# Turning early query and key tiles with 64x64 products, fewer halved first products, and a new step table, in a chunked attention + gated FFN kernel

## Chip, cores and metric

One NeuronCore of one Trainium2 chip runs the whole kernel. The metric is the device time of one execution in microseconds (us), from repeated runs; the kernel before takes 471.27 us (median of 3 runs, 470.78 to 471.43).

## What is computed

Batch 8, sequence 576, 8 heads of 64, model width 512, inner width 1024, all float32:

```python
def _attn_ref(q, k, v):              # attention inside chunks of 64 rows, 9 chunks a sequence
    scores = scale * np.matmul(q_c, k_c.transpose(0, 1, 2, 4, 3))
    scores = scores - np.max(scores, axis=-1, keepdims=True)
    attn = np.exp(scores)
    attn = attn / (np.sum(attn, axis=-1, keepdims=True) + 1e-09)
    out = np.matmul(attn, v_c)

def _moe_ref(x, w_in, conv_w, w_out):
    h = np.maximum(x @ w_in, 0.0)
    for k in range(K):               # a 3-tap convolution along the sequence, per inner feature
        conv_out += conv_w[k][None, None, :] * hp[:, k:k + S, :]
    gate = 1.0 / (1.0 + np.exp(-conv_out))
    return (h * gate @ w_out).astype(np.float32)
```

The attention output, heads side by side, is the `x` of the second function. `w_in`, `conv_w` and `w_out` reach the kernel as float64 and are split there.

## The kernel before

The 4608 rows are 36 tiles of 128 (two chunks each), and four tiles are a unit (9 units of 512 columns).

**Attention of a tile.** `load_rows` (L111) brings q and k, `t_pe` (L169) turns them on PE so that the 64 head features lie along partitions, `t_copy` (L189) brings the result from PSUM, `scores` (L206) multiplies, `s_max`, `s_sub`, `s_exp`, `s_sum`, `s_eps`, `s_rec`, `s_norm` (L222 to L275) make the softmax (DVE, with the exponential on ACT and the last product on POOL), `p_pe` and `p_copy` turn it, `attn_v` (L294) multiplies with v, and `x_hi`, `x_lo` (L325, L328) split the result into two fp32r parts, `x_h` and `x_l`. The first five tiles (t < `NP`) have q and k interleaved in one row buffer `r`: even partitions hold q, odd ones k, each partition two sequence rows. One step `t_pe` takes the rows of one parity (i is 0 or 1) of q and k: 8 products of 128 rows by 64 columns of weights over a 128-column stride-two view of the identity; two steps make a tile. Tiles 0 to 3 go through scores one by one, later ones in pairs.

**Feed-forward.** `mm1` (L332) makes 12 products per unit u and feature group f of 128 (8 groups) from `wi_h`, `wi_l`, `x_h`, `x_l`. Unit 0's are cut into two halves of 256 columns, so that the first half can begin when only tiles 0 and 1 are there. ReLU, the three taps (`c_mid`, `c_left` L378, `c_right` L384), the gate (`c_sig`, `c_mul` L394) and the split of the gated result (`g_hi`, `g_lo`) follow, then `mm2` (L465), three products for a block of 128 output rows and one f, stored by `o_store`.

**Weights.** `split` takes each float64 weight apart with `w_scale` (ACT), `w_shift` (L516) and `w_words` (L521) on DVE, `w_hi` (ACT, DVE L560 or POOL L563) and `w_left` (L525, DVE or POOL).

**Order.** Every operation is a step with an engine and assumed cost. A list of numbers, `order_`, gives the order in which the steps are laid out, and `moved_` puts some steps on another engine than their first. The code runs through the list with its assumed costs, hands out buffers and PSUM banks, emits the instructions, and then ties the order of each engine to what was emitted: every engine works strictly in that order, DMA issues (all on SP) too. Where that run leaves more than 0.7 us of the first 110 us between two PE steps, products of the identity with itself are put in (L1018 of 512 columns, L1021 of 128), into a bank that is free then. They compute nothing that is used.

## Time and profile before

| what | us |
|---|---|
| median of the runs | 471.27 |
| profiled execution | 470.57 |
| its span, first to last instruction | 468.8 |
| PE busy | 460.9 (98%) |
| DVE busy | 350.3 (75%) |
| ACT busy | 226.6 (48%) |
| POOL busy | 184.6 (39%) |

Busy time counts an instruction from its start to its modelled end. Matmuls overlap each other, so a group's busy sum on PE can exceed the time it takes; differences between start times show what a step takes. The profile counts each float32 product that goes through the array twice as two records: a step of 8 products in `t_pe` is 16 records, one of 16 products in `scores` 32.

### The profile page before, as it was taken

Reading aid. Unit: us, or ns where it says so; the run is one execution under the profiler, and the core shown is the slowest. Engines: PE = TensorE matmul, PEld = TensorE weight load, DVE = VectorE, ACT = ScalarE, POOL = GpSimd, SP = SyncE. Lnnn points to the kernel's source line nnn. Section 1 sums busy time; section 2 is a strip of 40 time slices with the busy share of each in tenths; the row PEclk is TensorE's granted clock in tenths of the full one; section 3 lists DMA queues with packets and bytes.
Section 4 is the critical chain, followed back from the end, with each engine's and each line's share of the span. In section 5 each row is a group of like instructions: output and inputs, shape, how many; then the busy total and the mean of one; then the engine's idle time right before and its main releaser. Section 6 shows DMA issues by size and latency. Waiting matters only on the chain.

```text
span 468.8 us, 10873 instructions
## 1 busy us (share of the span) xinstructions
PE 460.9 (98%) x4373; PEld 384.1 (82%) x4373; DVE 350.3 (75%) x632; ACT 226.6 (48%) x522; POOL 184.6 (39%) x256
## 2 busy tenths in 40 slices
PE   8999999999999999999999999999999999999996
PEld 6789978888888888888888888888888888888885
DVE  2999998699879947995997868894799178436630
ACT  3678964365347524651365435444355076115521
POOL 1224645067145630674064625272345246203230
PEclk9999999999999999999999999999999999999999
DMA  8998979957469514759496488602230103101002
GB/s 212 250 317 247 279 81 128 149 95 95 96 110 146 135 57 72 167 89 146 101 144 78 67 135 154 119 1 70 60 99 3 45 1 112 46 1 69 1 22 112
DMA packets 175638, 50.53 MB, mean 108 GB/s; under 512 B 159180, under 2 KB 167908, under 8 KB 175588
## 3 DMA queue, kind: packets, MB, share of 16 engines
q1 hardware_dynamic: 175588, 49.85, 55.4%
q8 instruction: 34, 0.56, 0.5%
q14 instruction: 16, 0.13, 0.1%
HBM read 36.72 MB, written 9.44 MB: 98 GB/s over the span
## 4 chain that ended last, share of the span: by engine, by line
PE 89%; DVE 9%; issue 2%; ACT 0%; POOL 0%; POOLq 0%; DVEq 0%; ACTq 0%
PE b_ps L469 42%; PE b_ps L337 37%; PE b_ps L215 3%; PE b_ps L303 3%; PE b_ps L176 2%; DVE wt L521 1%; DVE x_l L329 1%; DVE z L245 1%; DVE ww L521 1%; DVE m L225 1%; DVE wi_l L525 1%; DVE c L378 1%; DVE wt L516 1%; DVE e L229 1%; DVE c L394 1%
## 5 line engine op out<-in xcount | busy, mean ns | idle before, releaser
L469 PE MATMUL b_ps<-wo_h,g_h 128*128 128x512 f32 x288 | 113.8, 395 | 0.3 <-DVE x_l L329 0.3
L469 PE MATMUL b_ps<-wo_h,g_l 128*128 128x512 f32 x288 | 112.2, 390 | 0.0
L469 PE MATMUL b_ps<-wo_l,g_h 128*128 128x512 f32 x288 | 112.2, 390 | 0.0
L417 POOL TENSOR_TENSOR g_l<-c,g_h 128x510 fp32r<-128x510 f32 (+1 forms) x80 | 79.4, 998 | 75.4 <-DVE g_h L406 48.5
L378 DVE SCALAR_TENSOR_TENSOR c<-b_ps,cw,c 128x510 f32<-128x510 f32 x72 | 53.2, 740 | 37.4 <-ACT c L373 30.8
L337 PE MATMUL b_ps<-x_h,wi_h 128*128 128x512 f32 (+1 forms) x320 | 79.8, 371 | 0.0
L337 PE MATMUL b_ps<-x_l,wi_h 128*128 128x512 f32 (+1 forms) x320 | 78.8, 368 | 0.0
L337 PE MATMUL b_ps<-x_h,wi_l 128*128 128x512 f32 (+1 forms) x320 | 78.7, 368 | 0.0
L337 PEld LDWEIGHTS b_ps<-x_h,wi_h 128*128 128x128 f32 x320 | 56.5, 188 | 10.6 <-issue 0.3
L337 PEld LDWEIGHTS b_ps<-x_l,wi_h 128*128 128x128 f32 x320 | 56.9, 188 | 10.1
L337 PEld LDWEIGHTS b_ps<-x_h,wi_l 128*128 128x128 f32 x320 | 56.9, 189 | 10.0
L469 PEld LDWEIGHTS b_ps<-wo_h,g_h 128*128 128x128 f32 x288 | 54.0, 188 | 12.4 <-DVE x_l L329 0.7
L469 PEld LDWEIGHTS b_ps<-wo_h,g_l 128*128 128x128 f32 x288 | 54.1, 188 | 11.4
L469 PEld LDWEIGHTS b_ps<-wo_l,g_h 128*128 128x128 f32 x288 | 54.1, 188 | 10.7
L373 ACT ACTIVATE c<-b_ps,cw 128x510 f32<-128x510 f32 (+1 forms) x72 | 49.8, 693 | 23.0 <-DVE b_ps L348 19.1
L344 ACT ACTIVATE b_ps<-b_ps 128x512 f32<-128x512 f32 x56 | 32.4, 584 | 55.2 <-PE b_ps L337 54.7
L260 POOL TENSOR_TENSOR wt<-wt,z 128x512 f32<-128x512 f32 x28 | 29.2, 1050 | 75.7 <-DVE z L251 28.0
L390 ACT ACTIVATE c<-c 128x510 f32<-128x510 f32 (+1 forms) x72 | 45.5, 635 | 27.7 <-DVE c L384 27.4
L394 DVE SCALAR_TENSOR_TENSOR c<-c,b_ps 128x510 f32<-128x510 f32 (+1 forms) x72 | 48.6, 678 | 10.2 <-ACT c L390 8.1
L384 DVE SCALAR_TENSOR_TENSOR c<-b_ps,cw,c 128x510 f32<-128x510 f32 (+1 forms) x72 | 53.0, 740 | 1.6 <-ACT rim L363 0.4
L201 DVE STREAM_TRANSPOSE qkT<-qk 128x512 f32<-128x512 f32 (+1 forms) x60 | 37.9, 641 | 2.8 <-DMA qk<-in_k 1.5
L326 ACT CAST x_h<-b_ps 128x512 fp32r<-128x512 f32 x36 | 20.6, 590 | 39.6 <-PE b_ps L303 36.0
(99 smaller groups left out, 504.4 us busy)
## 6 DMA issues: line engine op xcount, KB each, us to landing
out<-os SPq DMA_DIRECT2D x35, 256.0 KB, 2.3
qk<-in_k SPq DMA_DIRECT2D x24, 288.0 KB, 6.8
qk<-in_q SPq DMA_DIRECT2D x24, 288.0 KB, 5.9
v<-in_v SPq DMA_DIRECT2D x25, 256.0 KB, 3.3
w<-in_moe_w_out SPq DMA_DIRECT2D x4, 1024.0 KB, 7.3
wt<-wt SPq DMA_DIRECT2D x56, 64.0 KB, 2.0
v<-in_v SPq DMA_DIRECT2D x20, 128.0 KB, 4.4
w<-in_moe_w_in SPq DMA_DIRECT2D x2, 1024.0 KB, 7.0
```

The lines of the kernel that those rows point to most:

```text
L201: nc.vector.transpose(out=turned(st)[:, i].rearrange("p g (n i) -> p g n i", i=32)[:, :, to:to + n], in_=groups[b, i][:, :, n0:n0 + n, :])
L260: nc.gpsimd.tensor_tensor(out=two(st, "to"), in0=two(st, "of"), in1=z, op=ALU.mult)
L326: nc.scalar.copy(out=x_view(t, x_h), in_=x_src(st))
L337: nc.tensor.matmul(banks[st["h"]][:, c0:c1], lhsT=wt[:, f // 2, kt, P * (f % 2):P * (f % 2) + P], rhs=xt[:, u % 2, kt, c0:c1], start=n == ...
L344: nc.scalar.activation(out=h, in_=h, func=AF.Relu)
L373: nc.scalar.mul(out=st["c"], in_=banks[st["h"]][:, i0:i0 + n], mul=cw[:, FT + f:FT + f + 1])
L378: nc.vector.scalar_tensor_tensor(out=c[:, a:n], in0=banks[st["h"]][:, i0 + a - 1:i0 + n - 1], scalar=cw[:, f:f + 1], in1=c[:, a:n], op0=AL ...
L384: nc.vector.scalar_tensor_tensor(out=st["c"], in0=banks[st["h"]][:, i0 + 1:i0 + 1 + n], scalar=cw[:, 2 * FT + f:2 * FT + f + 1], in1=st["c ...
L390: nc.scalar.activation(out=st["c"], in_=st["c"], func=AF.Tanh, scale=0.5)
L394: nc.vector.scalar_tensor_tensor(out=st["c"], in0=st["c"], scalar=1.0, in1=banks[st["h"]][:, i0:i0 + n], op0=ALU.add, op1=ALU.mult)
L417: nc.gpsimd.tensor_tensor(out=g_l[:, f, gs], in0=st["c"][:, cs], in1=g_h[:, f, gs].bitcast(F32), op=ALU.subtract)
L469: nc.tensor.matmul(banks[st["o"]], lhsT=gt[:, f, o:o + P], rhs=wt[:, f, :], start=f == 0 and n == 0, stop=f == FT - 1 and n == 2)
```

## The change

A step `t_pe64` replaces the two `t_pe` steps of tiles 0 to 4: q lies in partitions 0 to 63 and k in 64 to 127, each product takes a 64x64 block of one of them over a 64x64 identity, 32 products in all, q's into one PSUM bank and k's into another. `t_copy` reads the new layout. Unit 0's `mm1` is halved for groups 0, 1, 6 and 7 only. `s_eps`, the addition of 1e-9 on 128x8 values, may go to POOL (21 of 36 do). Assumed transfer times are changed, and `order_` and `moved_` are new throughout. Filler products differ where the gaps of the assumed run differ.

```diff
+    HALVED = (0, 1, 6, 7)
...
     def load_rows(st, t):
         if t < NP:
-            r = row_slot(st).rearrange("(p two) (h c) -> two p h c", two=2, h=H)
+            r = row_slot(st).rearrange("(two p) (h c) -> two p h c", two=2, h=H)
...
     def t_pe(st, i):
 
         tp = banks[st["tp", i]]
-        if st["t"] < NP:
-            r = row_slot(st).rearrange("p (g u e d) -> p g u e d", g=G, u=2, e=2)
-            for g in range(G):
-                for u in range(2):
-                    nc.tensor.matmul(tp[D * u:D * u + D, P * g:P * g + P], lhsT=r[:, g, u, i],
-                                     rhs=ident.rearrange("p (n two) -> p two n", two=2), start=True, stop=True)
-            return
...
+    def t_pe64(st):
+
+        r = row_slot(st).rearrange("p (g u e d) -> p g u e d", g=G, u=2, e=2)
+        for g in range(G):
+            for e in range(2):
+                for u in range(2):
+                    for i in range(2):
+                        nc.tensor.matmul(banks[st["tp", i]][D * u:D * u + D, P * g + C * e:P * g + C * e + C], lhsT=r[C * i:C * i + C, g, u, e],
+                                         rhs=ident[C * i:C * i + C, C * i:C * i + C], start=True, stop=True)
...
         if st["t"] < NP:
-            copy(out=qk.rearrange("p i g (n e) -> p e g i n", e=2)[:, i], in_=banks[st["tp", i]].rearrange("p (g i n) -> p g i n", g=G, i=2))
+            copy(out=qk[:, i].rearrange("p g (n e) -> p g e n", e=2), in_=banks[st["tp", i]].rearrange("p (g e n) -> p g e n", g=G, e=2))
             return
...
+    def s_eps_g(st):
+        nc.gpsimd.tensor_scalar(out=st["z"], in0=st["z"], scalar1=1e-9, scalar2=None, op0=ALU.add)
...
-        s = step("DVE", 0.17, key + 2, s_eps, (st,), [s], port=True)
+        s = step("DVE", 0.17, key + 2, s_eps, (st,), [s], port=True, alt=[dict(eng="POOL", cost=0.2, fn=s_eps_g, port=True)])
...
-        if u == 0:
+        if u == 0 and f in HALVED:
             s = step("PE", 1.43, key, mm1, (st, u, f, 0, UN // 2), wi_done[f] + [x_done[0], x_done[1]], take=[("bk", st, "h")])
             s = step("PE", 1.43, key, mm1, (st, u, f, UN // 2, UN), [s, x_done[2], x_done[3]])
         else:
...
     order_ = [
-        71, 72, 90, 0, 74, 91, 1, 73, 75, 3, 2, 77, 92, 78, 4, 5, 93, 109, 94, 110,
...
```

The rows below are the order in which an engine's instructions stand, equal ones that follow each other on one row; the number behind a buffer's name tells buffers apart, and a name after `<-` is read. They hold no times.

PE at the start, before: `r_108` to `r_111` are the row buffers of tiles 0 to 3, `qkT` a tile's turned q and k, `e` its softmax.

```order
L1018 MATMUL b_ps<-ident 128x512
L1021 MATMUL b_ps<-ident 128x128 x10
L176 MATMUL b_ps<-ident,r_108 64x128 x16
L176 MATMUL b_ps<-ident,r_109 64x128 x8
L215 MATMUL b_ps<-qkT_72 64x64 x16
L176 MATMUL b_ps<-ident,r_109 64x128 x8
L176 MATMUL b_ps<-ident,r_110 64x128 x8
L215 MATMUL b_ps<-qkT_73 64x64 x16
L176 MATMUL b_ps<-ident,r_110 64x128 x8
L578 MATMUL b_ps<-ident,wt_82 128x24
L176 MATMUL b_ps<-ident,r_111 64x128 x16
L284 MATMUL b_ps<-ident,e_76 128x128 x4
```

PE at the start, after the change:

```order
L1029 MATMUL b_ps<-ident 128x512
L1032 MATMUL b_ps<-ident 128x128 x5
L184 MATMUL b_ps<-ident,r_108 64x64 x32
L1032 MATMUL b_ps<-ident 128x128
L219 MATMUL b_ps<-qkT_72 64x64 x16
L184 MATMUL b_ps<-ident,r_109 64x64 x32
L1032 MATMUL b_ps<-ident 128x128 x2
L184 MATMUL b_ps<-ident,r_110 64x64 x32
L219 MATMUL b_ps<-qkT_73 64x64 x16
L585 MATMUL b_ps<-ident,wt_82 128x24
L184 MATMUL b_ps<-ident,r_111 64x64 x32
L291 MATMUL b_ps<-ident,e_76 128x128 x4
```

Tile 0's scores (first L215, now L219) stand directly behind tile 0's turn and a filler, where before half of tile 1's turn stood between.

DVE at its first instructions, before: `os` and `wt_82` belong to the split of the convolution's weights, `m` is a row maximum.

```order
L535 TENSOR_SCALAR wt_82<-os_70 24x128
L192 COPY qkT_72<-b_ps 128x4x2x64
L544 TENSOR_SCALAR wt_82<-os_70 24x128
L225 TENSOR_REDUCE m_74<-b_ps 128x8
L548 SCALAR_TENSOR_TENSOR wt_82<-os_70,wt_82 24x128
```

DVE at its first instructions, after the change:

```order
L196 COPY qkT_72<-b_ps 128x4x2x64
L542 TENSOR_SCALAR wt_82<-os_70 24x128
L551 TENSOR_SCALAR wt_82<-os_70 24x128
L229 TENSOR_REDUCE m_74<-b_ps 128x8
L233 TENSOR_TENSOR e_76<-b_ps,m_74 128x2x4x64
```

The copy of tile 0 stands ahead of the convolution's weights now. From the first row maximum (L225, now L229) to the eighth split of an attention result (`x_lo`, L329, now L336), the end of tile 7, DVE holds 97 instructions before and 92 after: without three `s_eps`, one `g_hi` (two casts), one `w_hi` of 512 columns and one `p_copy`, and with one `c_right` and one `c_mul` more; all others are the same in number.

PE around the first product of unit 1, before: the three rows of L337 are its 12 products, L469 are `mm2` products of unit 0. In the program L303 rows (`attn_v` of tiles 6 and 7) stand just ahead.

```order
L469 MATMUL b_ps<-wo_h,g_h 128x512
L469 MATMUL b_ps<-wo_l,g_h 128x512
L469 MATMUL b_ps<-wo_h,g_l 128x512
L337 MATMUL b_ps<-x_h,wi_h 128x512 x4
L337 MATMUL b_ps<-x_l,wi_h 128x512 x4
L337 MATMUL b_ps<-x_h,wi_l 128x512 x4
L469 MATMUL b_ps<-wo_h,g_h 128x512
```

The same place after the change:

```order
L476 MATMUL b_ps<-wo_h,g_h 128x512
L476 MATMUL b_ps<-wo_l,g_h 128x512
L476 MATMUL b_ps<-wo_h,g_l 128x512
L344 MATMUL b_ps<-x_h,wi_h 128x512 x4
L344 MATMUL b_ps<-x_l,wi_h 128x512 x4
L344 MATMUL b_ps<-x_h,wi_l 128x512 x4
L476 MATMUL b_ps<-wo_h,g_h 128x512
```

The neighbours are alike; ahead of this product stand five `mm2` steps of three products before and six after, so one has moved ahead of it.

On SP, the loads of tile 4 (four of `r_112`) move from behind tile 3's to behind the first `w_in` load and two v tiles; the first nine loads keep their places.

## Rows read from the trace of the kernel before

**Rows 1.** Stretches of the span: start and end, length, then the busy time of PE, PE's weight loads, DVE, ACT and POOL with their counts of instructions, the clock granted to PE, the mean share of the 16 DMA engines and the GB/s that they moved.

```profile
0.00:20.00 20.00, 18.55 (x341) 15.39 (x341) 10.25 (x26) 9.27 (x16) 3.45 (x10) 1.00 0.92 232
20.00:66.00 46.00, 43.25 (x629) 38.95 (x624) 45.57 (x77) 37.86 (x69) 20.20 (x23) 1.00 0.84 239
66.00:466.00 400.00, 399.14 (x3411) 329.73 (x3409) 294.51 (x531) 179.42 (x439) 161.00 (x224) 1.00 0.51 86
```

**Rows 2.** Two of PE's waits over the whole span: line that waited, engine and line it waited for, us in total, times, longest.

```profile
PE b_ps L284 <- POOL e L277: 1.5, 2, 0.9
...
PE b_ps L469 <- DVE x_l L329: 0.3, 1, 0.3
...
```

**Rows 3.** The chain of work that ended last, some pieces in order of time: start, us, what.

```profile
65.27 0.96 PE b_ps L469 x3
66.23 2.73 PE b_ps L337 x12
...
115.80 1.09 PE b_ps L215 x64
116.90 0.93 PE b_ps L303 x64
...
284.10 2.95 PE b_ps L337 x12
...
291.12 2.72 PE b_ps L337 x12
...
465.22 0.60 ACT os L474
```

**Rows 4.** DVE alone in two stretches: length, busy time (instructions), granted clock, DMA share, GB/s.

```profile
9.55:16.00 6.45, 5.76 (x17) 1.00 1.02 228
16.00:20.00 4.00, 3.54 (x7) 1.00 1.17 292
```

**Rows 5.** PE in order of time: start, us, line, what.

```profile
3.23 2.34 PE L1021 MATMUL b_ps<-ident 128*128 128x128 f32 x10
5.50 3.28 PE L176 MATMUL b_ps<-ident,r 128*64 128x128 f32 x48
8.71 0.70 PE L215 MATMUL b_ps<-qkT 64*64 64x64 f32 x32
...
35.52 0.64 PE L337 MATMUL b_ps<-x_h,wi_h 128*128 128x256 f32 x4
...
36.96 0.64 PE L337 MATMUL b_ps<-x_h,wi_h 128*128 128x256 f32 x4
```

**Rows 6.** DVE in order of time, some rows: start, us, line, what, and the idle time just ahead with what ended it.

```profile
7.90 0.67 DVE L192 COPY qkT<-b_ps 128x512 f32<-128x512 f32 x1
...
9.55 0.69 DVE L225 TENSOR_REDUCE m<-b_ps 128x8 f32<-128x512 f32 x1 [0.85 <-ACT qkT L192]
...
13.12 0.16 DVE L248 TENSOR_SCALAR z<-z 128x8 f32<-128x8 f32 x1
...
16.65 1.29 DVE L225 TENSOR_REDUCE m<-b_ps 128x8 f32<-128x512 f32 x2 [0.33 <-PE b_ps L215]
...
39.55 0.90 DVE L560 CAST wi_h<-ww 128x512 fp32r<-128x512 f32 x1
40.36 0.68 DVE L521 SCALAR_TENSOR_TENSOR wt<-wi,wt 128x512 uint32<-128x512 uint32 x1
...
48.80 0.49 DVE L406 CAST g_h<-c 128x127 fp32r<-128x127 f32 x2
49.20 1.27 DVE L394 SCALAR_TENSOR_TENSOR c<-c,b_ps 128x511 f32<-128x511 f32 x2
...
60.83 0.68 DVE L289 COPY pT<-b_ps 128x512 f32<-128x512 f32 x1
61.43 0.67 DVE L394 SCALAR_TENSOR_TENSOR c<-c,b_ps 128x511 f32<-128x511 f32 x1
62.04 1.22 DVE L525 TENSOR_TENSOR wo_l<-ww,wo_h 128x1024 fp32r<-128x1024 f32 x1
...
63.93 1.29 DVE L329 TENSOR_TENSOR x_l<-b_ps,x_h 128x512 fp32r<-128x512 f32 x2
65.13 0.74 DVE L384 SCALAR_TENSOR_TENSOR c<-b_ps,cw,c 128x511 f32<-128x511 f32 x1
65.79 0.74 DVE L378 SCALAR_TENSOR_TENSOR c<-b_ps,cw,c 128x510 f32<-128x510 f32 x1
```

**Rows 7.** The turns of tiles 0 to 4 (line 176) in the five stretches that they take: the sum over all.

```profile
sum 10.34, PE 10.24 PEld 8.98; mean PE 2.05 PEld 1.80
```

**Rows 8.** The time in which tiles 0 to 3, then v and the first weights arrive; columns as in Rows 1.

```profile
0.00:4.00 4.00, 2.64 (x6) 1.50 (x7) 0.00 (x0) 1.49 (x2) 1.36 (x8) 1.00 0.37 104
4.00:6.00 2.00, 2.00 (x16) 1.67 (x16) 0.00 (x0) 0.00 (x0) 0.00 (x0) 1.00 1.03 278
6.00:8.00 2.00, 1.91 (x34) 1.70 (x32) 0.25 (x2) 0.62 (x1) 0.00 (x0) 1.00 0.96 268
8.00:10.00 2.00, 2.00 (x58) 1.75 (x56) 1.15 (x3) 1.03 (x2) 0.00 (x0) 1.00 1.08 308
10.00:12.00 2.00, 2.00 (x59) 1.72 (x53) 1.93 (x8) 1.25 (x2) 0.00 (x0) 1.00 1.16 212
```

**Rows 9.** All filler products of 128 columns: ns at least, median, at most; first and last start.

```profile
L1021 PE MATMUL b_ps<-ident x16: 272/421/421, 3.2 to 47.9; 128*128 128x128 f32 x16
```

## The prediction, made before the changed kernel was run

> **What bounds the kernel now.** I read the stretches of the span first. From 66 us on PE is busy 399.14 of 400 us, so there the time is the sum of PE's work, and DVE has room (294.51 of 400). Before 66 us it is otherwise: from 20 to 66 us DVE is busy 45.57 of 46 us and PE 43.25 [rows 1]. PE's waits say the same: the last one of the whole span, at line 469, ended on `x_l`, DVE's split of tile 7's attention [rows 2]. Then the chain that ended last: it goes over to PE for good at 65.27 us, unit 1's first product starts at 66.23, and PE's last product ends at 465.22, 398.99 us later [rows 3]. So I split the time in two: how soon DVE gets through the first 65 us, up to the end of `x_l` of tile 7 at 63.93 + 1.29 = 65.22 [rows 6], and how much PE work is left behind unit 1's first product. PE work removed ahead of that point does not count by itself, since PE would only wait longer there.

> **PE work that the change removes.** The turns of tiles 0 to 4 take 10.34 us now, 2.07 a tile [rows 7]. No row shows `t_pe64`. The nearest are 32 products of 64x64 in `scores` and `attn_v`, which use the same quarters of the array in the same way: 1.09 us, or 0.93 straight behind others of that shape [rows 3]. I take 1.09 a tile; the bounds are 0.93 and the old 2.07. That is 10.34 - 5 x 1.09 = 4.9 us less. A halved first product takes 36.96 - 35.52 = 1.44 us a half [rows 5], a whole one 2.72 [rows 3]: 4 x (2 x 1.44 - 2.72) = 0.64 less. All 5.5 us lie before 66 us, where DVE is the limit, so they pay only through the terms below. The four uncut groups stand behind all of unit 0's attention anyway.

> **Term 1, DVE starts sooner: -1.2 us.** DVE's first row maximum starts at 9.55 after 0.85 us of waiting [rows 6], since tile 0's two turns and half of tile 1's stand ahead of its scores (48 records from 5.50, scores at 8.71, rows 5). Tile 0's turn keeps its start at 5.50: its loads are first as before, and the fillers ahead of it end at 5.57 now [rows 5], so fewer of them gain nothing that I can count on. After the change: turn to 6.59; both copies side by side, one on ACT and one on DVE, 0.14 later (the hand-over from scores to the maximum, 9.55 - 9.41) and 0.67 long [rows 6], to 7.40; scores 0.14 later and 0.70 long, to 8.24; maximum at 8.38. With the turn at 0.93 this term is -1.3, with 2.07 it is -0.2. The weights of the convolution, which DVE also does here, need about 0.4 us and fit in the gap.

> **Term 2, DVE has less to do: -0.9 us.** Between the first maximum and tile 7's `x_l` the order lists seven instructions fewer and two more. By start-to-start differences the removed ones cost 0.81 (`w_hi`), 0.60 (`p_copy`), 0.40 (the two casts of `g_hi`) and about 0.12 for each of three `s_eps`, 2.17 in all; the added `c_right` costs 0.66 and `c_mul` 0.61 [rows 6]. ACT and POOL take the removed ones over; they are busy 37.86 and 20.20 of the 46 us [rows 1]. The three `s_eps` on POOL stand between two DVE instructions of the same tile, so each could cost DVE a POOL instruction's wait, 20.20 / 23 = 0.9 us, if POOL is in the middle of one; the order puts the first on an idle POOL and other DVE work between the last two and their reciprocals. I take nothing for it and keep 2.6 as the bound.

> **Term 3, DVE's remaining idle time: -0.5 us.** From 9.55 to 20 us DVE idles 0.69 + 0.46 = 1.15 us [rows 4], waiting for tiles whose turn stood in PE's queue. Shorter turns give back some; 0 and 1.15 are the bounds, I take the middle, rounded down.

> **Term 4, the loads: +0.6 us.** q and k of a tile now go to 64 adjacent partitions each, where they were spread over all 128. By 10 us 0.42 + 0.56 + 0.54 + 0.62 = 2.12 MB have moved, which is tiles 0 to 3 [rows 8]. At some 300 GB/s the first bytes came at 2.6 us. Tile 0's 0.52 MB were through at 4.4 and its turn began at 5.50, so 1.1 us lie between. Tile 3 can then be turned at 11.1 and have its maximum 1.09 + 0.81 + 0.84 + 0.14 = 2.9 us later, at 14.0; terms 1 and 3 with one `s_eps` bring DVE there (16.65 now, rows 6) at about 14.85. So at the present rate the loads have 0.85 us to spare. No row shows such loads into adjacent partitions. The slowest nearby stretch moved 212 GB/s [rows 8], with smaller packets: then tile 3's maximum comes at 2.6 + 10.0 + 1.1 + 2.9 = 16.6, 1.7 late. Nothing and 1.7 are the bounds; I take a third. Tile 4's loads move behind two v tiles and a weight, and tile 5's behind them; their scores stand after 25 us in PE's order now, and I give them no price.

> [...]

> **Term 5, PE's rest behind unit 1's first product: -1.2 us.** Before, this product starts 1.01 us after `x_l` ends (66.23 - 65.22), because the wait stood at an `mm2` step ahead of it. After, six `mm2` steps stand ahead where five stood, and I let the product start 0.1 us after `x_l`: -0.9. One `mm2` step less remains: three products of 512 columns, 2.72 / 4 = -0.68. Counted in the order, 64x64 products and wide ones take turns once more behind this point: (1.09 - 0.93) + (2.95 - 2.72) = +0.4 [rows 3]. Has PE time for its work ahead of this? Before it had 66.23 - 5.50 = 60.7 us with some 2.7 of waiting; after, 60.7 - 2.7 - 5.5 + 0.7 = 53.2 us of work, fillers included, in the 57.8 us from 5.50 to 63.3. It has.

> **Sum.** DVE's end of `x_l`: 65.22 - 1.2 - 0.9 - 0.5 + 0.6 = 63.2. PE's end: 63.3 + 398.99 - 0.68 + 0.4 = 462.0, which is 3.2 us sooner. The stores behind it don't change. The profiled execution took 470.57 us, 0.70 less than the median of the runs, 471.27; so 467.4 for it and **468.0 us** as the median.

> **Rivals.** *The loads are slow* (0.20): 212 GB/s, term 4 is 1.7, the gain 2.1, 469.2 us. For it: the unfamiliar destination; against it: nothing but that the packets of these loads stay as large. [...] *All of PE's removed work is gained* (0.10): 5.5 us, 465.8 us. For it: PE is busy 98%, and a new order may feed it earlier. Against it: DVE's 45.57 of 46 us. *The tail eats it* (0.11): after 66 us PE has no waits now, but the order of all engines is new there. A wait then counts in full; one for a 1.22 us DVE instruction [rows 6] three times over takes 3.7 us, and the time is 471.3 or a little more or less. Against it: DVE has 105 us of room there. *Slower* (0.12): the loads fall to half, 139 GB/s. Tile 3's maximum then comes at 2.6 + 15.3 + 1.1 + 2.9 = 21.9 us, 7.0 late, and the kernel ends 7.0 - 3.8 = 3.2 us later, at 474.5. It turns from gain to loss where that maximum comes at 18.65, so below 2.12 MB in 12.1 us, 176 GB/s.

> [...]

> **How the numbers follow.** My forecast has 0.47 with a range of its own of 467.0 to 468.7 (2.6 to 4.3 us gained). With 466.2 to 470.6 the range takes in the slow loads, most of the case that all is gained, and the weak half of the tail case: 0.8. About 0.2% (0.9 us) is what a measurement of this kernel can tell from no change. Faster: 0.47 + 0.20 + 0.10 = 0.77; the tail case gives same, 0.11; slower 0.12.

> **What would show it.** Each `t_pe64` takes 64 records in about 1.1 us. The first maximum on DVE stands near 8.4 us, that of tiles 2 and 3 near 15.4, `x_l` of tile 7 ends near 63.2, and unit 1's first product starts just behind it. PE waits more than now before 63 us and not at all behind. I am wrong if tile 3's turn waits for a DMA beyond 12.5 us, if a turn costs near 2 us, or if PE waits in the tail.

## The result, and the profile after

The changed kernel takes 474.13 us in the median of 4 runs (473.36 to 474.32), the kernel before, on the same chip, 471.02 (4 runs, 470.45 to 471.43). The ratio is 1.0064, 95% interval 1.0046 to 1.0081: 3.0 us slower by the ratio, where 3.3 us less had been forecast. The profiled executions differ by 2.8 us in span, 471.6 against 468.8.

The stretches that answer to [rows 1], of the changed kernel; columns as there.

```profile
0.00:20.00 20.00, 13.42 (x391) 10.39 (x395) 7.29 (x19) 7.94 (x13) 3.39 (x11) 1.00 0.97 222
20.00:66.00 46.00, 42.63 (x680) 37.03 (x673) 44.58 (x73) 36.16 (x67) 19.52 (x22) 1.00 0.83 238
66.00:466.00 400.00, 400.00 (x3439) 330.47 (x3432) 293.56 (x512) 187.25 (x452) 167.59 (x242) 1.00 0.49 87
```

Behind 66 us PE is as full as before. The loss lies in the first 20 us: PE is busy 13.42 us there (18.55 before), and DVE 7.29 (10.25), though PE executes more records (391 against 341). PE's waits over the whole span, which answer to [rows 2], say on what it stood; columns: line that waited, what ended the wait, us in total, times, longest.

```profile
PE b_ps L184 <- issue: 2.5, 1, 2.5
PE b_ps L219 <- issue: 1.7, 2, 1.4
...
PE b_ps L184 <- DMA r<-in_k: 0.6, 1, 0.6
```

`L184` is the new turn, `L219` the scores. "Issue" means that the trace shows nothing that PE waited for: no semaphore, transfer or other engine was late. In order of time on PE (start, us, line, what, idle time just ahead), answering to [rows 5]:

```profile
5.69 1.98 PE L184 MATMUL b_ps<-ident,r 64*64 64x64 f32 x62 [0.60 <-DMA r<-in_k]
...
8.56 1.13 PE L219 MATMUL b_ps<-qkT 64*64 64x64 f32 x32 [0.48 <-DVE wt L542]
9.43 1.39 PE L184 MATMUL b_ps<-ident,r 64*64 64x64 f32 x64
...
11.29 1.03 PE L184 MATMUL b_ps<-ident,r 64*64 64x64 f32 x52
14.84 0.39 PE L184 MATMUL b_ps<-ident,r 64*64 64x64 f32 x11 [2.51 <-issue]
...
15.85 1.16 PE L184 MATMUL b_ps<-ident,r 64*64 64x64 f32 x64
...
17.53 0.46 PE L219 MATMUL b_ps<-qkT 64*64 64x64 f32 x15
19.39 0.93 PE L219 MATMUL b_ps<-qkT 64*64 64x64 f32 x49 [1.40 <-issue]
```

PE stops in the middle of tile 2's turn, behind 52 of 64 records, for 2.51 us, and again in the middle of the scores of tiles 2 and 3 for 1.40. A product in the middle of a step waits for no data: its neighbours had the same. Both pieces stand in the chain that ended last ("12.32 2.51 issue", "17.99 1.40 issue"). What DVE makes of it, in order of time, answering to [rows 6]:

```profile
9.82 0.69 DVE L229 TENSOR_REDUCE m<-b_ps 128x8 f32<-128x512 f32 x1 [1.16 <-PE b_ps L219]
...
15.86 0.69 DVE L229 TENSOR_REDUCE m<-b_ps 128x8 f32<-128x512 f32 x1 [2.30 <-PE b_ps L219]
...
20.39 1.29 DVE L229 TENSOR_REDUCE m<-b_ps 128x8 f32<-128x512 f32 x2 [1.29 <-PE b_ps L219]
...
67.61 1.29 DVE L336 TENSOR_TENSOR x_l<-b_ps,x_h 128x512 fp32r<-128x512 f32 x2
```

The maximum of tiles 2 and 3 starts at 20.39, where it was 16.65; `x_l` of tile 7 ends at 68.90, 3.68 us later than before. In the chain that ended last, unit 1's first product follows at 69.36:

```profile
69.36 2.73 PE b_ps L344 x12
```

The chain goes to ACT's last copy at 467.99, so 398.63 us are left behind that product (398.99 before, [rows 3]). DVE alone from its first maximum to the end of `x_l`, before and then after: length, busy time (instructions), granted clock, DMA share, GB/s.

```profile
9.55:65.22 55.67, 54.09 (x98) 1.00 0.88 242
```

```profile
9.82:68.90 59.08, 53.67 (x93) 1.00 0.83 232
```

DVE works 0.42 us less and idles 5.41 us in place of 1.58. That is the result in one line.

### The profile page after: what moved, and what is told of

Its sections match the earlier page's. It is cut to its first block, busy times and chain, and to the rows that moved or that the text cites. A ratio compares the mean times of both kernels' runs of the same rounds, so it can differ in the third digit from the quotient of the medians.

```text
span 471.6 us, 11096 instructions
## 1 busy us (share of the span) xinstructions
PE 458.0 (97%) x4487; PEld 379.1 (80%) x4487; DVE 346.1 (73%) x604; ACT 231.9 (49%) x532; POOL 190.5 (40%) x274
## 4 chain that ended last, share of the span: by engine, by line
PE 89%; DVE 5%; issue 2%; ACT 1%; POOL 1%; DMA 1%; SPq 0%; DVEq 0%; POOLq 0%; ACTq 0%
PE b_ps L476 42%; PE b_ps L344 38%; PE b_ps L219 4%; PE b_ps L310 3%; DVE m L229 1%; PE b_ps L184 1%; DMA r<-in_k 1%; DVE c L401 1%; DVE wt L528 0%; DVE e L233 0%; DVE x_l L336 0%; DVE ww L528 0%; POOL e L284 0%; DVE wt L523 0%; DVE z L249 0%
## 5 line engine op out<-in xcount | busy, mean ns | idle before, releaser
L344 PEld LDWEIGHTS b_ps<-x_l,wi_h 128*128 128x128 f32 x304 | 55.4, 188 | 10.8
L344 PEld LDWEIGHTS b_ps<-x_h,wi_l 128*128 128x128 f32 x304 | 55.4, 188 | 10.6
L344 PEld LDWEIGHTS b_ps<-x_h,wi_h 128*128 128x128 f32 x304 | 54.5, 188 | 11.4 <-DVE e L233 0.7
L380 ACT ACTIVATE c<-b_ps,cw 128x510 f32<-128x510 f32 (+1 forms) x72 | 49.7, 691 | 20.4 <-DVE b_ps L355 15.8
L413 POOL CAST g_h<-c 128x510 fp32r<-128x510 f32 (+2 forms) x20 | 11.7, 589 | 50.6 <-DVE c L401 50.6
```

Of the source, the lines that this page charges most:

```text
L344: nc.tensor.matmul(banks[st["h"]][:, c0:c1], lhsT=wt[:, f // 2, kt, P * (f % 2):P * (f % 2) + P], rhs=xt[:, u % 2, kt, c0:c1], start=n == ...
L380: nc.scalar.mul(out=st["c"], in_=banks[st["h"]][:, i0:i0 + n], mul=cw[:, FT + f:FT + f + 1])
```

## What PE waits for: instructions

The first wait begins behind 222 products and 223 weight loads, the next exactly 256 of these records later. The kernel after, from the start to inside the first gap, and from there to inside the second (the first two counts are PE's products and its weight loads):

```profile
0.00:13.00 13.00, 9.66 (x222) 7.11 (x223) 4.01 (x11) 4.15 (x7) 1.35 (x8) 1.00 0.96 190
13.00:18.50 5.50, 3.15 (x128) 2.68 (x128) 2.71 (x5) 2.33 (x5) 1.28 (x2) 1.00 1.02 306
```

And the trace has a DMA queue that carries instructions in packets of 16 KB (queue, kind: packets, MB, share of 16 engines):

```profile
q8 instruction: 35, 0.57, 0.5%
```

**Theory.** PE uses a block of 256 instructions faster than the next one comes. **Rivals:** the slow pace of tile 0's turn (1.98 us where later turns take 1.16); the loads into 64 adjacent partitions; the new order itself.

### One part taken from each side

**e1_fill**: ten fillers ahead of tile 0's turn, where five stood.

```diff
-            while idle and pe_free + 0.14 < begin[i] - SLACK:
+            while idle and pe_free + 0.14 < begin[i] - (SLACK if begin[i] > 6.0 else 0.0):
```

> The changed kernel with fillers up to the planned start of tile 0's turn (ten of 128 columns instead of five); nothing else differs. Pace theory (PE's first turns run at the slower pace because PE did less before them: tile 0's turn took 1.98 us, its scores 1.13): tile 0's turn falls to 1.1 us, DVE's first maximum from 9.82 to about 8.5, and if that is what the kernel lost, the end comes 1.3 us sooner, 472.8. Instruction theory (PE waits 2.51 and 1.40 us, about 256 PE instructions apart, for instructions that are not there yet): the turn may shorten, but tile 1's maximum stays near 15.9 and tiles 2 and 3's near 20.4, and the time stays within 0.5 of 474.1. Load theory (the tiles' rows come late at 224 GB/s): no change either, 474.1.

Measured: 474.67 us, ratio 1.0089 (1.0072 to 1.0106). Tile 0's turn takes 1.43 us now and the first maximum starts at 8.75, 1.1 sooner than in the changed kernel, but tiles 2 and 3's still starts at 20.52. The two stretches between the waits, columns as above:

```profile
0.00:13.00 13.00, 9.02 (x222) 6.81 (x223) 4.21 (x12) 4.28 (x7) 1.98 (x10) 1.00 0.95 190
13.00:19.00 6.00, 4.53 (x128) 3.79 (x128) 3.08 (x7) 3.27 (x6) 0.82 (x2) 0.72 1.08 305
```

PE gets through its work sooner and stops at the very same record, which now is record 47 of tile 2's turn and not 52, since five fillers more stand ahead. The pace of tile 0 is not the cause: what it gives is lost at the end of the block, and the time is no better than the changed kernel's (ratio 1.0064). (Behind the wait the granted clock is lower here, 0.72 in the mean of the second stretch, which takes a part of it too.)

**e2_wide**: the turn in 16 products of 64x64 weights over 128 columns, so 64 instructions a tile; loads and order as after the change. Part of the computation is left out.

```diff
-            for e in range(2):
-                for u in range(2):
-                    for i in range(2):
-                        nc.tensor.matmul(banks[st["tp", i]][D * u:D * u + D, P * g + C * e:P * g + C * e + C], lhsT=r[C * i:C * i + C, g, u, e],
-                                         rhs=ident[C * i:C * i + C, C * i:C * i + C], start=True, stop=True)
+            for u in range(2):
+                for i in range(2):
+                    nc.tensor.matmul(banks[st["tp", i]][D * u:D * u + D, P * g:P * g + P], lhsT=r[C * i:C * i + C, g, u, 0],
+                                     rhs=ident[C * i:C * i + C, :], start=True, stop=True)
```

> The changed kernel with tile 0 to 4's turn in 16 products of 64x64 weights over 128 columns in place of 32 over 64: the same columns through the array in half the instructions. It leaves out the odd rows of q and k of these tiles (zeros in their place), so that its time is that of half as many turn instructions, not of the full work. Instruction theory: PE's waits for nothing that the profile shows fall from 4.4 us before 31 us to under 1, tiles 2 and 3's maximum comes near 16.5 instead of 20.4, and the time falls by 3 to 4 us, to 470 to 471. Load theory: tile 3 still comes late, the maximum at 19 or later, 473 to 474. Pace theory: at most 1 us less, 473.

Measured: 471.15 us, ratio 1.0014 (1.0004 to 1.0023). No wait on issue is left; maxima at 8.81, 12.50 and 16.30, and `x_l` ends at 66.52, 2.4 us sooner than in the changed kernel. The turns of tiles 0, 1 and 3 take 1.08 to 1.10, in the range of the 32 products (1.16 where no wait cuts in); tile 2's takes 1.54, and tile 4's 2.48 with the granted clock at 0.50. Half the instructions are worth 0.50% by the two ratios (1.0064 and 1.0014), 2.4 us; the two intervals leave about 0.2% either way, an estimate. The array's columns are the same in both. A DVE wait of another kind appears, for the split of the first `w_in` load; the row of DVE and that of ACT ahead of it:

```profile
20.02 0.69 DVE L522 TENSOR_SCALAR wt<-wt 128x1024 uint32<-128x1024 uint32 x1 [1.63 <-ACT wt L518]
```

```profile
18.87 1.12 ACT L518 ACTIVATE wt<-w 128x1024 f32<-128x1024 f32 x1 [3.08 <-DMA w<-in_moe_w_in]
```

**e3_old**: the new order with the old turn (16 products of 128 rows) and the old spread loads.

```diff
+        for e in range(2):
+            for g in range(G):
+                for u in range(2):
+                    nc.tensor.matmul(banks[st["tp", e]][D * u:D * u + D, P * g:P * g + P], lhsT=r[:, g, u, e],
+                                     rhs=ident.rearrange("p (n two) -> p two n", two=2), start=True, stop=True)
```

> The changed kernel (its order, its four halved groups) with the turn and the loads of before: rows spread over all partitions, 16 products of 64x128 a tile, both steps emitted together. Instruction theory: a tile needs 64 PE instructions instead of 128, the long waits go, and although the turn costs 1 us more a tile the time is 470 to 471.5, that of the kernel before or better. Load theory: the same, since the loads are spread again. Order theory (the new order or the halving is what costs): 473 or more.

Measured: 471.2 us (469.91 to 472.67), ratio 1.0009 (0.9995 to 1.0023). No wait on issue either. So the new order without the new turn is the kernel before, within the measurement.

**e4_32**: the kernel before, with each turn product cut in two of 64 columns. Same columns through the array (2.16 us a tile where the granted clock is 1.00 and no wait cuts in, for 2.04 to 2.06), same loads, same order, 128 instructions a tile.

```diff
-                    nc.tensor.matmul(tp[D * u:D * u + D, P * g:P * g + P], lhsT=r[:, g, u, i],
-                                     rhs=ident.rearrange("p (n two) -> p two n", two=2), start=True, stop=True)
+                    for k_ in range(2):
+                        nc.tensor.matmul(tp[D * u:D * u + D, P * g + C * k_:P * g + C * k_ + C], lhsT=r[:, g, u, i],
+                                         rhs=ident.rearrange("p (n two) -> p two n", two=2)[:, k_], start=True, stop=True)
```

> The kernel before with each turn product of tiles 0 to 4 cut into two of 64 columns: 32 products a tile over the same columns, 128 PE instructions a tile as after the change; loads, order and buffers are those of before. Instruction theory: PE meets waits that the profile gives no cause for, 0.5 to 2.5 us before 20 us, and the time rises by 0.5 to 2.5, to 471.5 to 473.5; less than after the change because the same count of instructions is spread over twice the time. Load and order theories: nothing changes beyond the overhead of the smaller products, 471.0 to 471.4.

Measured: 474.79 us (473.61 to 477.81), ratio 1.0098 (1.0061 to 1.0135), so 4.6 us slower, and more than any theory had said. Next to the number of instructions it holds the 0.1 us a tile of the smaller products and a stretch of granted clock 0.50 behind the last wait, at 28 us. The profiled execution is the slowest of the four, 477.81. Its waits, and the three stretches between them:

```profile
PE b_ps L216 <- issue: 3.5, 2, 2.1
PE b_ps L177 <- issue: 2.3, 1, 2.3
```

```profile
0.00:14.00 14.00, 11.31 (x221) 9.49 (x221) 4.02 (x11) 4.29 (x7) 1.37 (x8) 1.00 0.85 218
14.00:20.50 6.50, 4.83 (x127) 4.29 (x127) 3.27 (x9) 2.88 (x5) 2.09 (x2) 1.00 0.93 251
20.50:26.00 5.50, 3.57 (x126) 3.12 (x127) 4.14 (x9) 3.01 (x5) 0.46 (x1) 1.00 0.95 282
```

442, 254 and 253 records; with PE's 6, 2 and 3 semaphore instructions in these stretches they are 448, 256 and 256: the same blocks in another program, with waits in the scores and in the old turn alike. So the waits don't need the 64x64 products.

Where the packets of the instruction queue lie, read from the trace's own DMA records, in us:

```
kernel    block crossed  packet lands  PE goes on
after         9.12          13.61         14.84
after        12.11          17.81         19.39
e1_fill       7.85          12.60         14.05
e4_32         8.88          13.41         14.74
e4_32        12.45          19.60         21.04
e4_32        19.35          25.52         26.87
before        9.35          12.36         16.06 (no wait)
before       16.05          20.84         22.25 (0.2 waited)
e7_mixfill   18.47          25.67         27.21 (no wait)
```

"Block crossed" is the time of the last record of the block ahead of the one that runs out. Where PE waited, it goes on 1.2 to 1.6 us after the packet has landed, and the packet lands 3.0 to 7.2 us after the crossing. That the crossing is what starts the fetch is inferred from these times; in the rows that follow a wait it can't be earlier than the landing just before (13.61 for 12.11), so those spans are too long by up to 1.5 us. By these rows a block has to last some 4 to 9 us in this stretch, an estimate. That the full data queues make the packets late is argued from the stretch (DMA share 0.97 in the first 20 us) and was not varied. Before, PE took 6.7 us for it (9.35 to 16.05); with 128 instructions a turn it took 3.0 (9.12 to 12.11).

### The loads, and what is left

**e5_adj**: the kernel before with the new loads alone.

```diff
-            r = row_slot(st).rearrange("(p two) (h c) -> two p h c", two=2, h=H)
+            r = row_slot(st).rearrange("(two p) (h c) -> two p h c", two=2, h=H)
...
-                                     rhs=ident.rearrange("p (n two) -> p two n", two=2), start=True, stop=True)
+                                     rhs=ident, start=True, stop=True)
```

> The kernel before with one part of the change alone: q and k of tiles 0 to 4 are loaded into 64 adjacent partitions each, and the turn's products take the plain identity; order and number of instructions stay. If these loads run at about 220 GB/s (224 to 231 in the changed kernel, 268 to 308 before) and that lies on the path, DVE's maximum of tiles 2 and 3 comes 0 to 1.7 us later or the first w_in split waits, and the time is 471.5 to 472.5 us. If the loads are hidden, the time is 470.6, as before. PE shows no waits on issue beyond those before, since its instructions are as many.

Measured: 472.19 us against 470.47, ratio 1.0032 (1.0020 to 1.0043), so 1.5 us. Four stretches that answer to [rows 8], and the rows of ACT and DVE where it is lost:

```profile
4.00:6.00 2.00, 1.38 (x12) 1.17 (x12) 0.00 (x0) 0.00 (x0) 0.00 (x0) 1.00 1.22 228
6.00:8.00 2.00, 1.75 (x32) 1.51 (x28) 0.00 (x0) 0.64 (x1) 0.00 (x0) 1.00 1.21 226
8.00:10.00 2.00, 1.84 (x52) 1.64 (x54) 0.95 (x3) 1.03 (x2) 0.00 (x0) 1.00 1.22 225
10.00:12.00 2.00, 1.93 (x41) 1.72 (x41) 1.95 (x6) 0.91 (x2) 0.00 (x0) 1.00 1.23 220
```

```profile
26.92 0.67 ACT L512 ACTIVATE wt<-wi 128x512 f32<-128x512 f32 x1 [1.43 <-DMA wi<-in_moe_w_in]
27.62 0.43 DVE L516 TENSOR_SCALAR wt<-wt 128x512 uint32<-128x512 uint32 x1 [1.37 <-ACT wt L512]
```

220 to 228 GB/s, where the spread loads moved 268 to 308 from 4 to 10 us [rows 8]. What makes these loads slower, no run shows. The 1.5 us lie near the upper bound of term 4, 1.7, which was worked out for 212 GB/s. But tiles 2 and 3 are late by only 0.46 (17.11 against 16.65), and the first maximum already by 0.47 (10.02 against 9.55). Most of the price falls later, on a `w_in` load that stands behind these in the queue: ACT waited 1.43 us for it, and DVE 1.37 for ACT. So the amount came near that bound on another path than the one it was worked out for: that is luck.

**e6_oldfill**: e3_old with ten fillers ahead of tile 0's turn (the edit of e1_fill).

> The changed kernel's order and halved products, with the old turns of 16 products of 128 rows, the old spread loads, and ten fillers of 128 columns ahead of tile 0's turn where five stood. Theory that PE's pace at the start is what is left of the loss without the instruction waits: tile 0's turn takes 2.2 us in place of 3.68, the first maximum stands at 9.3 to 9.6 in place of 10.55, and the time is 470.0 (469.4 to 470.5). Rival, that the new order itself costs this much elsewhere before 66 us: 471.2, as without the fillers.

Measured: 470.8 us, ratio 1.0002 (0.9993 to 1.0010). Tile 0's turn takes 2.04 us, the first maximum starts at 8.67, sooner than forecast for this run, and yet tiles 2 and 3's starts at 17.37. With turns of 2 us the order that was made for short ones keeps PE late from tile 1 on, so an earlier start is no gain. The time lies between the two theories' prices, and neither is shown.

**e7_mixfill**: 64x64 turns and adjacent loads for tiles 0 and 1 alone, ten fillers.

```diff
+        if st["t"] >= NQ:
...
+                        nc.tensor.matmul(banks[st["tp", e]][D * u:D * u + D, P * g:P * g + P], lhsT=r[:, g, u, e],
+                                         rhs=ident.rearrange("p (n two) -> p two n", two=2), start=True, stop=True)
+            return
```

> The changed kernel with 64x64 turns and adjacent loads for tiles 0 and 1 alone; tiles 2 to 4 are turned by the old 16 products from spread loads; ten fillers ahead of tile 0's turn. Theory that PE's instructions arrive in blocks of 256 and that a block wants some 6 us in this stretch: PE reaches the instruction at which it stalled (record 449) about 3 us later, so no wait on issue beyond 0.5 us near 12 us; first maximum at 8.75, that of tiles 2 and 3 at 16 to 17, time 469.9 (469.2 to 470.8). Rival, that the 64x64 turns cost by their form and not by their number: first stall stays near 11.3 to 12.3 us and the time is 472 or more.

Measured: 474.99 us, ratio 1.0093 (1.0080 to 1.0107). The forecast of this run failed: PE, quicker through the first tiles, came to the end of its block at 12.2 us and not 3 us later, the maximum of tiles 2 and 3 stands at 18.11 and not at 16 to 17, and the longest wait came five blocks further on. PE's waits, and the count up to the first:

```profile
PE b_ps L318 <- issue: 3.7, 2, 3.4
PE b_ps L227 <- issue: 1.3, 1, 1.3
```

```profile
0.00:13.00 13.00, 10.18 (x222) 7.86 (x223) 4.31 (x12) 5.08 (x9) 2.15 (x10) 1.00 0.96 224
```

The record is the same again, 222 + 223, and this time it lies in the scores of tile 1, behind an old turn. So the rival, that the form of the 64x64 products costs, falls although its price came out and its place nearly did; e4_32, without such products, speaks against it too. The wait of 3.42 us ends at 53.62, 1266 records and 14 semaphore instructions behind the first one, which is exactly five blocks. The block that runs out there begins at 47.6, just ahead of the scores and `attn_v` of two tiles, which use it up in 2.4 us.

**e8_widespread**: e2_wide with the old loads; both suspects gone.

> The changed kernel with 16 products a turn of 64x64 weights over 128 columns, and the old spread loads: both suspected costs, PE's instruction number and the slow loads, are taken away and all else of the change stays. Part of the computation is left out: the turned q and k are not the right rows. If those two costs are all that went wrong with the forecast, the time is 468.0 to 469.6 us (the forecast's 3.2 us of gain less the 0.6 it had set for loads, with its own uncertainty), tiles 2 and 3's maximum stands at 15.4 or sooner and DVE has no wait of 1.6 us for the first w_in split. If the order itself eats the gain, it stays at 470.5 to 471.2.

Measured: 469.99 us (468.91 to 471.24), ratio 0.9984 (0.9973 to 0.9995): 0.75 us faster than before, less than the 468.0 to 469.6 that was expected. With e2_wide this prices the parts, each against the kernel before on its chip: the order, halving, moved steps and the shorter turn together -0.16%, the loads +0.30%, the instructions +0.50%. (That these add up to the changed kernel's +0.64% follows from taking them as steps from one to the next.) Where the rest of the forecast's gain stays is seen in part, in a profile of 470.83 us, 0.84 above this kernel's median. Tiles 2 and 3's maximum starts at 16.28 and not at 15.4. DVE idles 3.37 us from its first maximum (9.25) to the end of `x_l` (66.34); 1.8 of them pass behind 48 us, where ACT waits for `w_out`:

```profile
ACT wt L518 <- DMA w<-in_moe_w_out: 1.7, 1, 1.7
ACT ww L518 <- DMA w<-in_moe_w_out: 1.6, 1, 1.6
```

In e6_oldfill only 0.2 us is waited there, at other landing times (5.0 us in the median of four, against 7.5), so this wait is not a fixed price. How much of the remaining 3 us (the forecast's 3.2 and the 0.6 set for loads, less 0.75) it holds, and how much the pace of the first turn (1.99 us in this profile, 1.10 for the same code in e2_wide), isn't settled.

No version that was run beats the kernel before by more than 0.16%, and that one leaves part of the computation out.

## Why the prediction was wrong

The sum of the forecast, with what the two profiles show:

| term | forecast | measured |
|---|---|---|
| 1, first maximum on DVE | -1.2 | +0.27 (9.82 against 9.55) |
| 2, DVE's work up to `x_l` | -0.9 | -0.42 |
| 3 and 4, DVE's idle time | +0.1 | +3.83 (5.41 against 1.58) |
| 5, PE behind `x_l` | -1.2 | -0.91 |
| sum | -3.2 | +2.8 |

**What bounds the kernel** was read rightly: `x_l` of tile 7 still sets the first part, PE the second, and no wait came in the tail.

**The step that failed** is "PE work that the change removes", with the sentence in term 5 that PE has time for its 53.2 us of work. Both priced the turn by the array (1.09 us a tile; where no wait cuts in, tile 3's took 1.16, tile 1's 1.39 and tile 4's 1.61) and never counted instructions: 128 a tile for 64, in a stretch where the DMA engines' share is 0.97. What the runs showed in its place: PE stands 2.51 and 1.40 us for instructions, and the number of instructions is worth +0.50%, 2.4 us (changed kernel against e2_wide). The two waits are 3.9 us and the idle time grew by 3.83, but that is a chance agreement: in e2_wide, without such waits, DVE still idles 4.11 us (57.71 from its first maximum to the end of `x_l`, 53.60 busy). The rows to see it stood in the profile of before, an instruction queue and a wait on issue, and no rival named it:

```profile
q8 instruction: 34, 0.56, 0.5%
PE b_ps L284 <- issue: 0.2, 1, 0.2
```

**What this explains.** From 3.3 us less to 3.0 us more are 6.3 us. The instructions are 2.4 of them and the loads, 1.4 for 0.6, another 0.8. The other 3 us are gain that isn't there in e8_widespread either. In its profile `x_l` ends at 66.34, where the sum without loads gives 62.62: 0.90 later at the first maximum, 0.53 more of DVE's work, 2.29 more of its idle time. Why that idle time didn't fall (term 3) stays open, but for the 1.8 us behind 48 us.

**Term 1** failed at PE's pace at the start: with five fillers tile 0's turn took 1.98 and its scores 1.13, where the sum has 1.09 and 0.70, and the turn began at 5.69. That is 0.9 + 0.4 us, and the rows to see it are those of the fillers: 421 ns in the median and 272 at best [rows 9]. The granted clock of 1.00 that the views print there is no record (last section). e1_fill shows that it didn't decide.

**Term 2** was half: start-to-start differences had priced the removed instructions too high, or the others grew; busy time fell by 0.42.

**Term 4**: a third of the bound was the wrong choice. e5_adj measures 1.5 alone, e2_wide less e8_widespread 1.4; in the changed kernel itself the loads ran at 220 to 231 GB/s from 4 to 12 us. The place was wrong too: for the most part not tile 3's turn (in e2_wide it waits 0.55 us for its rows, to 13.46), but the first weights behind the tiles. In e2_wide, where no instruction is late, DVE waits 1.63 us at 20.02 for them.

**Term 5** was nearly right: 398.63 us left (398.7 forecast), and the product 0.46 behind `x_l` for the 0.1 assumed. In the rivals, 468.0 and the 3.7 us of a wait in the tail make 471.7, not 471.3; nothing rested on it.

**The slower rival** had the sign, but not the cause: loads at 139 GB/s would have been needed, and they ran at 220 to 231. The mark "a turn costs near 2 us" was met for tile 0 alone; first maximum, tiles 2 and 3 and `x_l` stand at 9.82, 20.39 and 68.90, where 8.4, 15.4 and 63.2 would have shown the forecast right.

## To carry to other kernels

Count instructions, not only array time, before a product is cut into smaller ones: a float32 product here is four on PE (two products and two weight loads in the trace), they came 256 at a time, and in the first 30 us of this kernel, with a DMA share of 0.97 in the first 20, a block had to last some 4 to 9 us, an estimate from the table above. Here a wait that the profile put down to "issue" in the middle of a row of equal products, 256 instructions or a multiple of that after another, was that, and five fillers added ahead moved it from record 52 of tile 2's turn to record 47. A slower load was paid here less by the tile it brings (0.46 us) than by what stands behind it in the queue (1.37 us). And before a granted clock of 1.00 is believed at the start of a span, compare the length of equal products there and later: here 418 ns and 269 for the same product, both at a printed 1.00 (below).

## What the runs showed that was not expected

- PE stood for up to 3.4 us where instructions were late, and stood at the same record (222 products and 223 loads) in three programs.
- The kernel before is itself near that edge: its block landed at 20.84 us and was used at 22.25, after a wait of 0.2.
- The granted clock reads 1.00 in the first 10 us of all these runs, yet the same turn of tile 0 took 1.10 us in e2_wide and 1.99 in e8_widespread, and 3.68 in e3_old against 2.04 in e6_oldfill. The traces settle it. Their own clock records begin only at 5.1 us in e2_wide, 9.1 in e8_widespread, 9.8 in e3_old, 4.2 in e6_oldfill, 10.0 in the changed kernel, 5.1 in e1_fill and 5.5 in the kernel before; ahead of the first record the view prints 1.00 for want of one. What the clock was there can be told by equal products. First, e8_widespread's turn of tile 0, printed at 1.00 with no record; then the same line of e2_wide, tile 4's turn, where records say 0.50, and tile 0's, behind the first record (ns at least, median, at most; below each its stretch, the granted clock being the third number from the end):

```profile
L183 PE MATMUL b_ps<-ident,r x32: 417/418/473, 5.1 to 6.7; 64*64 64x128 f32 x32
5.00:7.20 2.20, 2.08 (x33) 1.78 (x33) 0.06 (x1) 0.02 (x1) 0.00 (x0) 1.00 0.94 266
L183 PE MATMUL b_ps<-ident,r x30: 417/417/471, 22.2 to 23.8; 64*64 64x128 f32 x30
22.30:24.20 1.90, 1.90 (x31) 1.57 (x32) 1.74 (x5) 1.13 (x2) 0.00 (x0) 0.50 0.89 238
L183 PE MATMUL b_ps<-ident,r x30: 269/269/320, 5.8 to 6.7; 64*64 64x128 f32 x30
6.00:6.90 0.90, 0.90 (x31) 0.73 (x27) 0.00 (x0) 0.00 (x0) 0.00 (x0) 1.00 1.21 221
```

  So the first products ran at the pace of a granted clock of 0.50 (418 ns a product in the median, 417 in e2_wide where the records say 0.50), and the pace changes where the records begin: in the changed kernel a product of the turn takes 311 ns from 9.3 to 10.0 us and 218 from 10.1 on (medians). The fillers of 421 ns in the kernel before [rows 9] are the same case: the ten ahead of 5.5 us take 421, the six behind 272 to 328, and e2_wide's last four take 421 at 0.50. With five fillers the records begin at 5.1 to 10.0 us, with ten at 4.2 to 7.6; e2_wide and e8_widespread have the same fillers there and differ by 4 us, so the first maximum of one profile holds a share of luck.
- At or behind long waits of PE the clock fell too: in e1_fill to 0.50 from 16 to 18 us, behind a wait of 2.56 us, and tile 3's turn takes 1.84 us there (1.16 in the changed kernel). The same is on record in e2_wide (22 us, behind a wait of 2.07), e4_32 (28 us, behind 2.27) and e7_mixfill (53 us, behind 3.42), so their times hold some of it. In the profile of the changed kernel it stays at 1.00 behind a wait as long (2.51 us); its three other executions have means of 0.992 to 0.996, so in them it fell somewhere.
